# Logarithm of both parities of w, summed on TensorE, for steps 1 and 2 of a chunked RWKV kernel

## The chip, the cores and the metric

The kernel runs on one core of one Trainium2 chip. The metric is the device time of one execution in microseconds (us), as the median of several runs. A profile is one execution with the hardware profiler on. Engines are called by the profile's names: PE is TensorE (PEld its weight loads), ACT is ScalarE, DVE is VectorE, POOL is GpSimd, SP is the queue that issues all DMAs.

## The reference, cut to what matters

```python
# r, k, v, w: (4, 8, 768, 48), u: (8, 48); w lies between 0.8 and 0.95
for t in range(S):
    cur = einsum('bhd,bhe->bhde', u * k[t], v[t])
    y[:, :, t] = einsum('bhd,bhde->bhe', r[t], state + cur)
    state = w[t][..., None] * state + einsum('bhd,bhe->bhde', k[t], v[t])
x = y.transpose(0, 2, 1, 3).reshape(3072, 384)
out = maximum(x @ w_in, 0) ** 2 @ w_out      # w_in (384, 2048), w_out (2048, 384)
```

It is a linear attention with a decaying state for each head, and behind it a two-layer network with a squared ReLU. All inputs and the output are float32.

## The kernel before, in words

The sequence is worked on in 12 steps of 256 positions (4 batches of 3 steps). In a step two neighbouring positions (the two parities, j = 0 and 1) share one of 128 partitions, so a raw tile such as `w_raw` is 128 partitions x 8 heads x 2 parities x 48. The 256 positions of a step fall into two chunks of 64 partitions (c = 0 and 1).

What a step s does, by the names of its operations:

- `ww_` (line 272) multiplies the two parities of w, on the engine that the order names; `lw_` (line 276) takes the logarithm of the product on ACT into one of two buffers `lw_buf`, bf16, padded from 48 to 64 columns a head (the padding is zeroed once by POOL, lines 246 and 248).
- `cum_` (lines 332 to 336) sums the logarithms over the positions on PE: four small matmuls with two columns, which give the decay of a whole chunk, and two of 384 columns with triangular matrices. From step 3 on the second of these is left out, and `al_` on DVE derives it from the first; steps 0 to 2 do without `al_`. `exp_` (line 348) takes the exponential in PSUM, and `ac_` (line 354) that of the chunk decays.
- `rw_` and `kw_` (lines 294 and 298) move r and k by one parity, with POOL in the first steps. `rd_.s.1` (line 369, one instruction) and `rd_.s.0` (line 366, two halves) multiply k and r by the decays on DVE. `tr_` (line 382) transposes them on PE, and `rkt_` (line 396) copies them out of PSUM as kT (1) and rT (0).
- `p_` (line 422 or 425) multiplies kT and rT, `pm_` (lines 438 and 441) masks the product on DVE. `su_` (line 453), `ts_` and `sn_` (lines 461 to 468) carry the state on. `y_` and `yc_` (lines 490 and 502) make the output.
- The bonus term: `ku_` (line 305) is u times k, `qp_` (line 310) times r, `q_` (line 315) its sum, `qs_` and `vs_` (line 285) put that sum and v into rows of chunks, `vq_` (line 324) multiplies them, and `ysb_` (line 513) adds that to y. `v_` (line 280) casts v.
- The network: `yt_` and `xt_` (lines 525 and 530) transpose y, `m1_` (line 545) is the first layer, `rl_` (lines 554 and 556) the ReLU on ACT or DVE, `sq_` (lines 562 and 564) the square, `m2_` (line 576) the second layer, `os_` and `store` the output. `cast` (line 201) turns the loaded weights to bf16.
- `warm_.n.i.x` (line 596) issues n matmuls of 512 columns whose result nobody reads, into bank i.

The whole order of the work is written out by hand in the string `ORDER`. Its words are run one after the other: a word is an operation with its step, `=V`, `=A` or `=G` names DVE, ACT or POOL, and `:0`, `:m` and so on the PSUM banks. Every engine takes its own instructions strictly in that order; semaphores are set between engines where data or banks demand it. The loads of a step and of the weights are words too, and SP issues them in that order. PSUM has two pairs of banks for the attention (`att`), two banks `bk` and two banks `m1`.

Steps 0, 1 and 2 of the attention run at the start, ahead of the first `m1_`; what PE does between their operations there is `warm_`. From the first `m1_` on, attention and network are interleaved.

Of the kernel before, what the change touches and what calls it, by code (L numbers as in the profile page):

```python
# [22 lines left out]
ww_.2=G rkt_.1.1=A vs_.1.0=A lw_.2 v_.1=G y_.0:0 yc_.0.1 warm_.2.3.22 p_.1.1:1 p_.1.0:m warm_.6.1.7 vq_.0=G pm_.1.1
cum_.2:1 vs_.1.1=A pm_.1.0 qs_.1=A exp_.2 warm_.4.1.8 su_.1:m kw_.2=G ysb_.0=V rw_.2=G ts_.1.0=V warm_.1.0.23 y_.1:0
rd_.2.1 yc_.1.0 rd_.2.0 yt_.0:1 xt_.0=V sn_.1.0 cast.i.1=A vq_.1=G ts_.1.1=V warm_.1.0.24 tr_.2.1:2 yc_.1.1 ld.2.v
tr_.2.0:0 m1_.0.3:1 rkt_.2.1=A m1_.0.2:2 ac_.2 ysb_.1=V yt_.1:3 rkt_.2.0=A sn_.1.1 p_.2.1:1 rl_.0.3=A cast.i.0=V
p_.2.0:0 xt_.1=A ku_.2=V m1_.0.1:0 vs_.2.1=G m1_.1.0:3 m1_.1.2:1 vs_.2.0=A rl_.0.1=A m1_.1.1:0 v_.2=G rl_.0.2=A
rl_.1.0=A rl_.1.2=A qp_.2=G pm_.2.1 pm_.2.0 su_.2:1 rl_.1.1=V ts_.2.0=V ld.2.i m1_.0.0:2 m1_.1.3:1 cast.i.2=A y_.2:1
q_.2 yc_.2.0 sn_.2.0 yc_.2.1 rl_.1.3=A m1_.0.5:3 ld.3.i m1_.1.5:1 ld.3.w m1_.0.4:0 rl_.0.0=A rl_.0.5=V qs_.2=A
rl_.1.5=A cast.i.3=G m1_.1.7:3 ld.0.o m1_.1.4:1 vq_.2=V ysb_.2=V rl_.0.4=A rl_.1.7=A ww_.3=G cast.o.0=G m1_.0.7:2  # L30
yt_.2:3 ld.2.o m1_.0.6:0 lw_.3 cast.o.2=G cum_.3:1 xt_.2=V rl_.0.7=V ld.3.o m1_.2.4:3 rl_.0.6=V sq_.0.1=A ld.1.o
sq_.0.0=A rl_.1.4=A m1_.2.2:2 sq_.0.2=A m1_.1.6:0 m1_.2.7:1 ld.3.r rl_.1.6=A sq_.1.1=A rl_.2.2=V rl_.2.4=V m1_.2.5:2
rl_.2.7=V ld.3.k al_.3 rl_.2.5=V cast.o.1=V m1_.2.6:0 m2_.0.1.0:3 m2_.0.1.2 sq_.1.3=V kw_.3=G m1_.2.3:1 sq_.1.0=A
ld.3.v ld.5.w m2_.0.0.0:2 ac_.3 ld.4.w ld.4.r sq_.0.3=A rl_.2.6=A exp_.3 vs_.3.1=G ld.4.v ld.4.k m1_.2.0:0 m2_.0.0.2
m2_.0.1.1 cast.o.3=V rl_.2.0=A m1_.2.1:0 rw_.3=V m2_.0.1.3 rl_.2.3=A sq_.2.3=A rl_.2.1=A sq_.1.2=A rd_.3.0 m2_.0.0.1
os_.0.1=A tr_.3.0:0 rd_.3.1 m2_.0.0.3 tr_.3.1:1 ku_.3=V m2_.1.0.1:3 sq_.2.1=A os_.0.0=A m2_.1.0.0 rkt_.3.0=V
rkt_.3.1=V p_.3.0:0 v_.3=G p_.3.1:b su_.3:1 sq_.2.2=A vs_.3.0=A qp_.3=V ld.5.k ts_.3.0=A m2_.2.0.1:2 m2_.1.0.3
m2_.2.0.3 m2_.1.0.2 sq_.2.0=A ww_.4=G q_.3 pm_.3.0 lw_.4 qs_.3=A cum_.4:0 m2_.2.0.0 ld.6.w v_.4=A pm_.3.1 ww_.5=G
rw_.4=G sn_.3.0 ts_.3.1=V vq_.3=G ac_.4 al_.4 m2_.2.0.2 yc_.3.1:1 y_.3 m2_.2.1.0:1 m2_.2.1.2 os_.1.0=A kw_.4=V lw_.5
ysb_.3=V sn_.3.1 store.0.0 os_.2.0=A exp_.4 kw_.5=G rd_.4.1 rd_.4.0 cum_.5:1 ac_.5 yt_.3:3 xt_.3=A ld.5.r vs_.4.0=A  # L40
al_.5 store.0.1 ld.6.r m2_.2.1.3 m2_.2.1.1 os_.2.1=V m1_.3.0:3 rl_.3.0=A exp_.5 su_.4:0 m1_.3.1:2 rl_.3.1=A
m2_.1.1.3:0 m2_.1.1.1 dtr_.4.1 ku_.4=V rw_.5=V qp_.4=V m1_.3.7:2 rl_.3.7=A m1_.3.6:1 ts_.4.0=V dtr_.4.0 rl_.3.6=A
m2_.1.1.2 m1_.3.5:3 rd_.5.1 rl_.3.5=A m1_.3.4:1 sn_.4.0 ts_.4.1=V p_.4.0:0 q_.4 rd_.5.0 qs_.4=A ww_.6=G vs_.4.1=G
vq_.4=G rw_.6=G p_.4.1:1 sq_.3.0=V m2_.3.1.0:3 m2_.1.1.0 pm_.4.0 yc_.4.1:0 yc_.4.0 sq_.3.3=A m1_.3.3:2 rl_.3.4=A
sq_.3.2=A pm_.4.1 y_.4 lw_.6 m1_.3.2:1 rl_.3.3=A rl_.3.2=A cum_.6:1 m2_.3.0.2:2 m2_.3.0.3 sq_.3.1=A m2_.3.1.3
m2_.3.1.1 ku_.5=G qp_.5=G ld.5.v ysb_.4=V al_.6 ld.7.w ld.6.k ww_.7=G yt_.4:1 m2_.3.1.2 m2_.3.0.0 exp_.6 ac_.6
os_.1.1=V sn_.4.1 m2_.3.0.1 kw_.6=V rd_.6.0 rd_.6.1 dtr_.5.1 ld.6.v v_.5=G dtr_.5.0 xt_.4=A p_.5.1:1 store.2.0 ld.7.r
vs_.5.1=A os_.3.1=A lw_.7 su_.5:b p_.5.0:0 q_.5 v_.6=A store.2.1 ts_.5.0=V m1_.4.1:1 ku_.6=G rl_.4.1=A vs_.6.0=A
m1_.4.3:0 os_.3.0=A pm_.5.0 pm_.5.1 rl_.4.3=V m1_.4.2:3 rl_.4.2=A vs_.6.1=A qs_.5=G m1_.4.4:1 sn_.5.0 yc_.5.1:0
yc_.5.0 rl_.4.4=V su_.6:1 dtr_.6.0 m1_.4.7:0 rl_.4.7=A vs_.5.0=G dtr_.6.1 y_.5 m1_.4.6:1 ts_.6.0=V sn_.6.0 ld.9.w  # L50
m1_.4.5:3 m1_.4.0:2 vq_.5=V sq_.4.1=A rl_.4.6=A rl_.4.5=A sq_.4.2=A ysb_.5=V ts_.6.1=V rl_.4.0=V sq_.4.0=V yt_.5:0
m2_.4.1.1:1 xt_.5=A qp_.6=G q_.6 qs_.6=G ld.7.k p_.6.0:1 ld.8.v p_.6.1:m yc_.6.1:0 ld.7.v ld.8.r store.1.1 ld.8.w
vq_.6=G ku_.7=G pm_.6.1 sq_.4.3=A kw_.7=G m2_.4.1.0 m2_.4.1.2 m1_.5.1:0 rl_.5.1=A pm_.6.0 m2_.4.1.3 sn_.6.1 m1_.5.0:2
cum_.7:1 y_.6 m1_.5.7:3 vs_.7.0=A rl_.5.0=A os_.4.1=A ww_.9=V al_.7 m2_.4.0.0:0 rl_.5.7=V m1_.5.2:2 m1_.5.6:1 ww_.8=G
rw_.7=G exp_.7 ac_.7 m2_.4.0.1 vs_.7.1=G m2_.4.0.2 m1_.5.3:3 rl_.5.2=A sq_.5.0=A v_.7=A rl_.5.3=A m1_.5.5:2 sq_.5.1=A
ysb_.6=V vs_.8.0=G m2_.4.0.3 lw_.8 rl_.5.6=A rd_.7.1 qp_.7=V rd_.7.0 sq_.5.3=A su_.7:0 v_.8=G rl_.5.5=V rw_.8=V
m1_.5.4:3 rl_.5.4=V m2_.5.1.0:2 cum_.8:1 sq_.5.2=A ts_.7.0=V al_.8 q_.7 m2_.5.1.1 m2_.5.1.3 store.1.0 ld.8.k ld.11.k
ac_.8 store.3.1 dyt_.6 dtr_.7.1 dtr_.7.0 exp_.8 kw_.8=V sn_.7.0 ts_.7.1=V m1_.6.2:3 m2_.5.1.2 m1_.6.3:1 ld.9.r ld.10.w
sn_.7.1 os_.4.0=A rd_.8.1 m1_.6.1:0 os_.5.1=A ku_.8=G m1_.6.7:2 rd_.8.0 rl_.6.2=V ld.9.k rl_.6.3=A qs_.7=A m1_.6.4:1
su_.8:1 rl_.6.7=A p_.7.1:m p_.7.0:0 qp_.8=G rl_.6.1=V ts_.8.0=V yc_.7.1:1 yc_.7.0 rl_.6.4=A sq_.6.1=A m2_.5.0.2:0  # L60
m1_.6.6:1 store.3.0 rl_.6.6=A sq_.6.3=A dtr_.8.1 pm_.7.0 pm_.7.1 lw_.9 dtr_.8.0 m2_.5.0.1 m1_.6.5:2 y_.7 m1_.6.0:3
m2_.5.0.3 m2_.5.0.0 store.4.1 ku_.9=G q_.8 qs_.8=G ww_.10=G rl_.6.5=V vq_.7=V rl_.6.0=A vs_.8.1=A rw_.9=G sq_.6.0=A
p_.8.0:m p_.8.1:0 kw_.9=G qp_.9=G ysb_.7=V cum_.9:1 m2_.6.0.1:1 ld.9.v os_.5.0=A m2_.6.0.3 m2_.6.1.3:0 m2_.6.0.0
sq_.6.2=V m2_.6.0.2 m2_.6.1.0 sn_.8.0 al_.9 exp_.9 pm_.8.0 rd_.9.0 pm_.8.1 ld.10.k dyt_.7 v_.9=A ac_.9 m1_.7.7:2
y_.8:0 yc_.8.1 rd_.9.1 su_.9:1 vs_.9.1=A yc_.8.0 rl_.7.7=A m1_.7.4:3 ld.10.v vq_.8=G ysb_.8=V m1_.7.0:2 lw_.10
store.4.0 q_.9 rl_.7.4=A ts_.9.0=A rl_.7.0=A cum_.10:0 al_.10 vs_.9.0=V ac_.10 exp_.10 m2_.6.1.1 os_.6.0=V m2_.6.1.2
os_.6.1=A m1_.7.5:2 m1_.7.6:3 m1_.7.2:0 kw_.10=G dtr_.9.0 qs_.9=G rl_.7.5=A ld.10.r dyt_.8 sq_.7.2=A m1_.7.3:2
m1_.7.1:1 rl_.7.6=A dtr_.9.1 ld.11.w m1_.8.5:3 rl_.7.3=A rl_.7.1=A m1_.8.6:2 v_.10=G sn_.9.0 ts_.9.1=V rw_.10=G
rd_.10.1 rd_.10.0 ku_.11=G rl_.7.2=A rl_.8.5=V sq_.7.1=A ld.11.v m1_.8.7:1 p_.9.0:1 p_.9.1:0 m1_.8.1:3 store.6.1
vq_.9=G ww_.11=G ld.11.r vs_.10.1=G store.6.0 pm_.9.0 sn_.9.1 rl_.8.6=A rl_.8.7=A rl_.8.1=A lw_.11 m2_.7.1.2:0  # L70
m2_.7.1.1 pm_.9.1 kw_.11=V m1_.8.3:2 y_.9:0 yc_.9.1 su_.10:1 ysb_.9=V dtr_.10.0 m1_.8.4:1 sq_.7.3=A sq_.7.0=A
m2_.7.1.3 cum_.11:0 m2_.7.1.0 ts_.10.0=V rw_.11=V rl_.8.4=A rl_.8.3=V dtr_.10.1 ku_.10=G sq_.8.2=A ac_.11 os_.7.1=A
# [577 lines left out]
```

## Time and profile before

| | |
|---|---|
| median of 3 runs | 178.65 us (178.42 to 179.02) |
| the profiled execution's own time | 178.38 us |
| its span, first to last instruction | 176.6 us |
| busy in the span | PE 171.2, DVE 138.4, ACT 134.0, POOL 110.0 us |
| granted TensorE clock | full in all 40 slices of the span |

Busy times are sums of instruction durations. In a timeline line stand the start, the duration (from the first start to the last end, where several instructions are merged), the engine, the line, what is written from what, the count, and, in brackets, the idle time of the engine just before it with what ended it. The difference between span and time, 1.78 us, lies ahead of the first instruction and behind the last.

### The profile page before, as it was taken

To read this page: it belongs to the slowest core of one execution; us is meant where nothing else is said; L and a number is where in the kernel's file an instruction comes from. 1 tells how busy PE (TensorE), PEld (TensorE's weight loads), DVE (VectorE), ACT (ScalarE), POOL (GpSimd) and SP (SyncE) were. 2 spreads that over 40 slices of the span, in tenths; PEclk is the share of its full clock that TensorE was granted. 3 is DMA by queue.
4 is the path that set the end of the run, shared out by engine and by line. 5 is a ranking of instruction groups with operands and counts; after the bars stand their busy time and mean duration, and the time that the engine had idled before them with its cause. 6 is when DMAs were issued, how large, how long until landed. Compare 5 with 4: busy or idle time off the path is not lost.

```text
span 176.6 us, 5525 instructions
## 1 busy us (share of the span) xinstructions
PE 171.2 (97%) x2296; PEld 124.7 (71%) x2296; DVE 138.4 (78%) x205; ACT 134.0 (76%) x240; POOL 110.0 (62%) x132
## 2 busy tenths in 40 slices
...
GB/s 140 262 261 265 304 352 344 366 346 253 262 261 284 123 147 234 183 282 256 276 266 159 234 234 234 186 198 163 298 138 126 105 29 17 106 59 89 89 4 134
DMA packets 78954, 35.61 MB, mean 202 GB/s; under 512 B 72145, under 2 KB 77394, under 8 KB 78930
## 3 DMA queue, kind: packets, MB, share of 16 engines
...
## 4 chain that ended last, share of the span: by engine, by line
PE 91%; DVE 3%; DMA 2%; ACT 1%; issue 1%; DVEq 0%; ACTq 0%
PE m L545 19%; PE m L576 18%; PE bk L576 18%; PE bk L545 17%; PE att L490 3%; DMA w_raw<-in_w_dram 2%; PE m L596 2%; PE att L502 2%; PE att L453 2%; PE att L425 2%; PE bk L596 2%; DVE ww L272 1%; PE att L334 1%; PE bk L382 1%; PE att L332 1%
## 5 line engine op out<-in xcount | busy, mean ns | idle before, releaser
L545 PEld LDWEIGHTS <-wi_sb 128*128 128x128 bf16 x576 | 54.8, 98 | 10.0 <-DMA xT<-y_sb 0.2
L576 PEld LDWEIGHTS <-gt 128*128 128x128 bf16 x400 | 37.7, 98 | 19.5 <-ACT gt L562 0.2
L545 PE MATMUL m<-xT,wi_sb 128*128 128x256 bf16 x300 | 39.4, 273 | 0.0
L562 ACT ACTIVATE gt<-gt 128x1024 bf16<-128x1024 f16 x37 | 38.2, 1052 | 0.5
L545 PE MATMUL bk<-xT,wi_sb 128*128 128x256 bf16 x276 | 36.5, 273 | 0.0
L576 PE MATMUL bk<-wo_sb,gt 128*128 128x384 bf16 (+2 forms) x208 | 36.0, 314 | 0.0
L576 PE MATMUL m<-wo_sb,gt 128*128 128x384 bf16 x192 | 35.0, 326 | 0.0
L554 ACT ACTIVATE gt<-m 128x512 f16<-128x512 f32 x32 | 18.8, 595 | 11.0 <-PE m L545 10.6
L554 ACT ACTIVATE gt<-bk 128x512 f16<-128x512 f32 x36 | 21.0, 596 | 7.6 <-PE bk L545 7.4
L556 DVE TENSOR_SCALAR gt<-m 128x512 f16<-128x512 f32 x18 | 12.3, 687 | 13.0 <-PE m L545 12.6
L441 DVE TENSOR_TENSOR pmT<-att,mask 128x1024 bf16<-128x1024 f32 x16 | 19.1, 1215 | 1.1 <-PE att L425 0.9
L324 POOL TENSOR_TENSOR ku<-v_sh,qs 128x768 f32<-128x768 bf16 x9 | 13.3, 1475 | 8.6 <-ACT qs L285 8.5
L468 POOL TENSOR_TENSOR S<-t_state,ac_buf 128x192 bf16<-128x192 f32 x20 | 11.9, 595 | 10.0 <-DVE t_state L463 9.0
L305 POOL TENSOR_TENSOR ku<-k_raw,u_bc 128x768 f32<-128x768 f32 x9 | 16.7, 1855 | 0.6 <-DMA k_raw<-in_k_dram 0.6
L298 POOL TENSOR_TENSOR k_raw<-k_raw,w_raw 128x384 f32<-128x384 f32 x8 | 8.0, 1005 | 9.9 <-DMA k_raw<-in_k_dram 9.9
L513 DVE TENSOR_TENSOR y_sb<-att,ku 128x768 bf16<-128x768 f32 x12 | 11.5, 954 | 3.5 <-PE att L490 1.5
L369 DVE TENSOR_TENSOR kdec_buf<-k_raw,att 128x768 bf16<-128x768 f32 x12 | 11.4, 947 | 3.1 <-ACT att L348 3.1
L285 ACT CAST v_sh<-v_raw 64x384 bf16<-64x384 f32 x26 | 13.2, 509 | 0.3
L310 POOL TENSOR_TENSOR ku<-ku,r_raw 128x768 f32<-128x768 f32 x7 | 12.7, 1809 | 0.2
L366 DVE TENSOR_TENSOR rdec_buf<-r_raw,att 128x384 bf16<-128x384 f32 x24 | 12.2, 544 | 0.4 <-POOL r_raw L294 0.4
L285 POOL CAST v_sh<-v_raw 64x384 bf16<-64x384 f32 x18 | 10.6, 589 | 1.4 <-DMA v_raw<-in_v_dram 0.5
L315 DVE TENSOR_REDUCE q<-ku 128x16 f32<-128x768 f32 x12 | 11.3, 944 | 0.1
...
## 6 DMA issues: line engine op xcount, KB each, us to landing
...
kT<-kdec_buf SPq DMA_TRANSPOSE x8, 4.6
```

Source lines behind the costliest of these rows:

```text
L285: copy(out[j * Q:(j + 1) * Q, c], src[c * Q:(c + 1) * Q, :, j])
L305: tensor_mul("ku_", s, h)(tiles["ku", s][:, hs], raw["k", s][:, hs, 1:3, :], u_bc[:, hs, None, :].to_broadcast([C, n, 2, D]))
L310: tensor_mul("qp_", s, h)(ku, ku, raw["r", s][:, heads(h), 0:2, :])
L324: tensor_mul("vq_", s)(vq[:], tiles["vs", s][:], tiles["qs", s][:, :, :, None].to_broadcast([C, 2, H, D]))
L366: nc.vector.tensor_mul(rdec[0][:, ps, j, :, 0:D], x[:, :, j, :].rearrange("p (a e) d -> p a e d", e=2), dec.rearrange("p (a e) d -> p a e ...
L441: nc.vector.tensor_mul(pmT, ps_p[:].rearrange("p e (x t) -> p (e x) t", t=C), mk.to_broadcast([C, 8, C]))
L468: nc.gpsimd.tensor_mul(t[:], tiles.pop(("ts", s, c))[:].rearrange("p (a d) -> p a d", a=HP), tiles["a_c", s][:, :, c, None].to_broadcast([ ...
L545: nc.tensor.matmul(ps1[:, j, :], wi_sb[:, n // 4, kk, n % 4 * 128:(n % 4 + 1) * 128], tiles["xT", s][:, :, kk, :], start=(kk == 0), stop=( ...
L554: nc.scalar.activation(rl, m1, AF.Relu, scale=RS)
L556: nc.vector.tensor_scalar(out=rl, in0=m1, scalar1=RS, scalar2=0.0, op0=ALU.mult, op1=ALU.max)
L562: nc.scalar.activation(gt, rl, AF.Square)
L576: nc.tensor.matmul(m2, gt[:, 4 * q + n, rows * C:(rows + 1) * C], wo_sb[:, 4 * q + n, cols], start=(summed[s, c] == 1 and n == 0), stop=(s ...
```

## The change

Steps that have an `lw_` but no `ww_` in the order now take the logarithm of both parities in one ACT instruction, into one buffer `lw_pair` that steps 1 and 2 share, and each matmul of `cum_` becomes two, one for each parity, which add up in PSUM. `ww_.1` (on DVE) and `ww_.2` (on POOL) are gone. POOL zeroes `lw_pair` among the constants.

```diff
+    PAIR_LN = {steps with an lw_ word} - {steps with a ww_ word}
+    lw_pair = consts.tile([C, 2, H, DP], BF16)
         nc.gpsimd.memset(lw_bufs[1][:], 0.0)
+        if PAIR_LN:
+            nc.gpsimd.memset(lw_pair[:], 0.0)
     def lw_(s, h=None):
+        if s in PAIR_LN:
+            nc.scalar.activation(lw_pair[:, :, :, 0:D].rearrange("p j h d -> p h j d"), raw["w", s][:], AF.Ln)
+            return
     def cum_(s, h=None):
+        logs = [lw_pair[:, j] for j in range(2)] if s in PAIR_LN else [lw_bufs[s % NLW][:]]
...
         for p in pairs(h):
-            nc.tensor.matmul(cs[:, 0, DM + 2 * p:DM + 2 * p + 2], lw[:, 2 * p:2 * p + 2, :],
-                             half_ones[:], start=True, stop=True)
-        nc.tensor.matmul(cs[:, 0, 0:n], tri_strict[:], lw[:, hs, 0:D], start=True, stop=True)
-        if s not in ONE_SUM:
-            nc.tensor.matmul(cs[:, 1, 0:n], tri_incl_neg[:], lw[:, hs, 0:D], start=True, stop=True)
+            for lw, start, stop in zip(logs, ends["start"], ends["stop"]):
+                nc.tensor.matmul(cs[:, 0, DM + 2 * p:DM + 2 * p + 2], lw[:, 2 * p:2 * p + 2, :],
+                                 half_ones[:], start=start, stop=stop)
+        for into, tri in sums:
+            for lw, start, stop in zip(logs, ends["start"], ends["stop"]):
+                nc.tensor.matmul(into, tri[:], lw[:, hs, 0:D], start=start, stop=stop)
```

The order itself changes at these words and no others; between them it is the same:

| word | before | after |
|---|---|---|
| `ku_.0` | POOL, after `rw_.0` | DVE, after `rd_.0.0` |
| `ww_.1=V`, `ww_.2=G` | there | gone |
| `warm_.3.5.2` | after `rd_.0.0`, ahead of `tr_.0.0` | after `rd_.0.1`, ahead of `tr_.0.1` |
| `ac_.0` | after `p_.0.1`, behind `v_.0` on ACT | ahead of `rkt_.0.0` |
| `warm_.2.3.21` | between `tr_.1.0` and `tr_.1.1` | ahead of `warm_.5.5.3` and `p_.0.0` |
| `exp_.1` | after `vs_.0.0` on ACT | ahead of it (a cast of v) |
| `rd_.1.0`, `rd_.1.1` | in this order | the other way round |
| `vs_.1.0` | ACT | POOL |
| `vs_.1.1` | ahead of `qs_.1` on ACT | behind it |
| `warm_.1.0.23` | behind `su_.1` | ahead of `warm_.6.1.7` and `cum_.2` |
| `warm_.1.0.24` | ahead of `tr_.2.1` | ahead of `su_.1` |
| `warm_.4.1.8` | ahead of `su_.1` | behind it, ahead of `y_.1` |
| `qs_.2` | behind `rl_.0.0` | ahead of it |
| `m1_.3.3` | behind `m2_.3.1.0`, `pm_.4.0`, `yc_.4.1`, `yc_.4.0` | ahead of them |
| `rl_.6.5` | DVE | ACT |

More of the change, by code (lines that the diff above doesn't have):

```diff
@@ L23 @@
[L23 to L72, printed above, removed]
```

96 lines of the change are left out of this document (75 added, 21 removed).

## The prediction, on record before the run

> **What bounds the kernel now.** I read the page first, for busy shares, then the busy time by stretches, then the chain of waits, then the timeline of the first 27 us.
>
> ```profile
> span 176.6 us, 5525 instructions
> PE 91%; DVE 3%; DMA 2%; ACT 1%; issue 1%; DVEq 0%; ACTq 0%
> ```
> ```profile
> 25.00:30.00 5.00, 5.00 (x63) 4.37 (x61) 5.00 (x7) 4.94 (x10) 4.60 (x6) 1.00 1.09 361
> 100.00:105.00 5.00, 4.94 (x113) 4.04 (x111) 4.54 (x8) 4.00 (x9) 4.31 (x4) 1.00 1.22 261
> ```
> ```profile
> 9.21 1.59 DVE ww L272
> 25.29 0.71 PE bk L545 x6
> 103.05 0.36 DVE t_state L463
> ```
>
> The second line is the chain that ended last: 91% of it is PE. The stretch from 25 to 30 us has PE busy all 5.00 of 5 us at the full clock, and the one from 100 to 105, the only stretch between 15 and 170 us that is not full, still 4.94 (the chain puts the hole down to `ts_.8.0` at 103.05). So from the first `m1_` on, near 25.2, PE runs its own instructions back to back to the end. The edits of steps 1 and 2 lie ahead of that. They matter only by when the first `m1_` starts; the rest, 176.6 - 25.2 = 151.4 us, follows it one to one. The chain says where a gain could come from: `ww_.1` stands in it with 1.59 us, on DVE.
>
> **The change part by part. DVE.** These rows carry it.
>
> ```profile
> 3.12 0.53 POOL L248 MEMSET lw_buf<- 128x512 bf16 x1
> 4.56 0.56 DVE L272 TENSOR_TENSOR ww<-w_raw 128x384 f32<-128x384 f32 x1 [0.80 <-DMA w_raw<-in_w_dram]
> 8.58 1.81 POOL L305 TENSOR_TENSOR ku<-k_raw,u_bc 128x768 f32<-128x768 f32 x1
> 9.12 1.68 DVE L272 TENSOR_TENSOR ww<-w_raw 128x384 f32<-128x384 f32 x1
> 10.72 0.94 DVE L310 TENSOR_TENSOR ku<-ku,r_raw 128x768 f32<-128x768 f32 x1
> 12.21 1.01 POOL L298 TENSOR_TENSOR k_raw<-k_raw,w_raw 128x384 f32<-128x384 f32 x1 [1.82 <-DMA k_raw<-in_k_dram]
> ```
>
> The same product took 0.56 us alone and 1.68 while POOL worked on `ku_.0` (8.58 to 10.39). Removed: 1.59 us of DVE's chain. Added: `ku_.0` on DVE, of the size and type of `qp_.0` at 0.94, so 0.95. POOL's next work, `kw_.1`, waits for a DMA until 12.21, so nothing stands beside `ku_.0` there. DVE is 1.59 - 0.95 = 0.64 us earlier up to its next wait.
>
> The new memset of `lw_pair` is twice the size of the one at 3.12, so 2 x 0.53 = 1.06, from 3.65 to 4.71 on POOL, which has nothing to do then; it reaches 0.15 us into `ww_.0`, which is on the chain. If the two exclude each other that costs 0.15, else nothing; I take nothing, as the memsets at 3.12 kept their 0.53 beside DVE's own. [...]
>
> **ACT and PE up to p_.1.1.**
>
> ```profile
> 7.17 1.04 PE L596 MATMUL att<-warm 128*128 128x512 bf16 x4
> 8.33 0.62 PE L382 MATMUL bk<-ident,kdec_buf 128*128 128x128 bf16 x8
> 8.98 1.01 ACT L396 COPY kT<-bk 128x1024 bf16<-128x1024 bf16 x1 [1.24 <-PE bk L382]
> 10.08 1.01 ACT L396 COPY rT<-bk 128x1024 bf16<-128x1024 bf16 x1
> 10.99 0.83 ACT L280 CAST v_bf<-v_raw 128x768 bf16<-128x768 f32 x1
> 11.79 0.52 ACT L276 ACTIVATE lw_buf<-ww 128x384 bf16<-128x384 f32 x1
> 12.37 0.25 PE L332 MATMUL att<-half_ones,lw_buf 128*128 128x2 bf16 x4
> 12.64 0.32 PE L336 MATMUL att<-lw_buf,tri_incl_neg 128*128 128x384 bf16 x1
> 13.52 0.79 ACT L348 ACTIVATE att<-att 128x768 f32<-128x768 f32 x1
> 13.77 1.21 DVE L441 TENSOR_TENSOR pmT<-att,mask 128x1024 bf16<-128x1024 f32 x1
> 14.90 1.01 DVE L366 TENSOR_TENSOR rdec_buf<-r_raw,att 128x384 bf16<-128x384 f32 x2
> 15.82 0.95 DVE L369 TENSOR_TENSOR kdec_buf<-k_raw,att 128x768 bf16<-128x768 f32 x1
> 16.83 0.62 PE L382 MATMUL m<-ident,kdec_buf 128*128 128x128 bf16 x8
> 17.48 1.01 ACT L396 COPY kT<-m 128x1024 bf16<-128x1024 bf16 x1 [0.44 <-PE m L382]
> 18.56 0.40 PE L422 MATMUL att<-rT,kT 64*128 64x128 bf16 x8
> 19.28 1.21 DVE L441 TENSOR_TENSOR pmT<-att,mask 128x1024 bf16<-128x1024 f32 x1
> 19.12 1.47 PE L596 MATMUL bk<-warm 128*128 128x512 bf16 x6
> 22.30 0.39 PE L596 MATMUL bk<-warm 128*128 128x512 bf16 x1
> ```
>
> One warm matmul of 512 columns costs PE (1.47 - 0.39) / 5 = 0.216 us; 384 columns are then 0.16 and 128 are 0.054, by estimate. The four warms at 7.17 occupy PE to 8.03. `warm_.3.5.2` ahead of `tr_.0.1` keeps it to 8.68, where the transposes began at 8.33: 0.35 late. The kT copy goes from 8.98 to 9.33. Before, ACT idled some 0.1 us between its two copies, so the rT copy, `v_.0` and `ac_.0` (the last now first) slip by only 0.16, from the start of the rT copy to that of `lw_.1` still 11.79 - 10.08 = 1.71: `lw_.1` starts at 11.95 instead of 11.79.
>
> It has 768 elements now: bounded by 0.52 (no longer than with 384) and 1.04 (twice that); the cast of 128x768 beside it took 0.83, and I take that. It ends at 12.78, 0.47 later than before (12.31). That it no longer waits for `ww_.1` (done at 10.80) is worth nothing, since ACT came to it only at 11.79. `cum_.1` took 12.37 to 12.96, of which the four small matmuls and the first large one cost 0.27 of issue; six more cost 0.27 + 0.16 = 0.43 (bounds: nothing, and 0.59 again). So it ends at 12.78 + 0.06 + 0.59 + 0.43 = 13.86, and `exp_.1`, now ahead of `vs_.0.0`, starts at 13.90 instead of 13.52 and ends at 14.69. Moving it ahead is worth about 0.06 against before, where it waited for the cast, and the longer sum takes more than that.
>
> DVE is done with `pm_.0.1` at 14.90 - 0.64 = 14.26, and waits for `exp_.1` until about 14.78: 0.52 of its 0.64 are gone. The two decays last 15.82 + 0.95 - 14.90 = 1.87, to 16.65. `rd_.1.1` is first now, but PE's order still has `tr_.1.0` first, which needs the last half of `rd_.1.0`: seven transposes from 16.71, 0.38, and only then `tr_.1.1`, from 17.09 to 17.71, where it ended at 17.45 before. The kT copy, 17.74 to 18.75, and `p_.1.1` at 18.82: 0.26 later than 18.56. `pm_.1.1` starts when `p_.1.1` ends, at 19.28, as before. DVE's chain behind it, to `xt_.0`, keeps its place.
>
> **PE from p_.1.1 to the first m1_.**
>
> ```profile
> 20.55 0.24 PE L332 MATMUL att<-half_ones,lw_buf 128*128 128x2 bf16 x4
> 22.61 0.56 PE L490 MATMUL att<-v_sh,pmT 128*128 128x48 bf16 x16
> 24.61 0.68 PE L382 MATMUL bk<-ident,rdec_buf 128*128 128x128 bf16 x8
> 25.19 0.82 PE L545 MATMUL bk<-xT,wi_sb 128*128 128x256 bf16 x6
> ```
>
> Before, this took 25.19 - 18.56 = 6.63 us. PE waited in it three times: 0.13 before `cum_.2` (six warms from 19.12 end at 20.42, it began at 20.55, when `pm_.1.1` had read the bank), 0.09 before `y_.1` (22.30 + 0.22 to 22.61), and about 0.1 within `tr_.2.0` (0.58 from 24.61 to 25.19 against 8 x 0.054). The number of warms in it is 12 before and after; they are only dealt out otherwise, `warm_.4.1.8` behind `su_.1`. With `p_.1.1` late the three waits close, and `cum_.2` adds 0.43: 18.82 + 6.63 - 0.32 + 0.43 = 25.56 instead of 25.19. PE has then no slack left and sets the start of `m1_` itself, 0.37 late.
>
> **POOL and what comes later, at nothing.**
>
> ```profile
> 18.24 1.00 POOL L272 TENSOR_TENSOR ww<-w_raw 128x384 f32<-128x384 f32 x1
> 19.96 1.48 POOL L324 TENSOR_TENSOR ku<-v_sh,qs 128x768 f32<-128x768 bf16 x1
> 26.07 1.69 POOL L285 CAST v_sh<-v_raw 64x384 bf16<-64x384 f32 x2
> 105.34 0.60 ACT L554 ACTIVATE gt<-bk 128x512 f16<-128x512 f32 x1 [1.05 <-PE bk L545]
> ```
>
> POOL loses `ww_.2` (1.00) and gains `vs_.1.0`, two casts: at most 1.69, as at 26.07. What is queued behind is `v_.1`, `vq_.0`, `kw_.2`, `rw_.2`. `vq_.0` ended at 21.44 and DVE's `ysb_.0` needs it; at 1.69 it would come up to 0.69 late, DVE's chain with it, and by that chain the first `m1_` up to 0.5 late, a little more than PE's own 0.37. I take the casts as equal to `ww_.2`. `qs_.2` ahead of `rl_.0.0` and `m1_.3.3` ahead of `m2_.3.1.0` exchange work on engines where PE waits for nothing; `rl_.6.5` goes to ACT, which idled 1.05 there (105.34). If that cover is gone, each costs at most one instruction, 0.6.
>
> The sum: +0.37 us. From the profiled execution's 178.38 (span 176.6 and 1.78 around it) that is 178.75; the median, 178.65, lies 0.27 above that execution, so I forecast **179.0**. A measurement of this kernel can tell about 0.3%, 0.54 us, from no change, and 0.37 is under it.
>
> **Rivals.** *Faster: DVE stays the bound.* If the logarithm and the doubled sums cost near their lower bounds (0.52 and little), `exp_.1` ends by 14.17, DVE keeps its 0.64, and PE follows: 178.65 - 0.64 = **178.0**. For it: DVE has no idle time in the trace from 7.3 to 30 us, and `ww_.1` is in the chain. Against: it needs more than 0.52 of the 0.31 + 0.43 that I add on ACT and PE to be unreal. Chance 0.2.
>
> *Slower: the doubled sums at their upper bounds.* PE between `p_.1.1` and `m1_` has no slack once `p_.1.1` is later than about 18.5, and from there every delay of the path `lw_.1`, `cum_.1`, `exp_.1`, `tr_.1.1` goes through whole. With 1.04 for the logarithm (+0.21) and 0.59 for each doubled sum (+0.16 on the path and +0.16 again behind `p_.1.1`) that gives 0.37 + 0.53 = 0.90: **179.6**. It decides from +0.17 over my sum on. For it: the path has many small handovers, each of which I set at what it was before. Chance 0.35.
>
> *The change doesn't do what it says:* if `cum_` hides in PE's idle time and the words moved cancel, 178.65; that lies within my own case, whose chance is 0.45 with all that ends within 0.3%, its own range 178.3 to 179.2.
>
> **How the numbers follow.** The time is my own case's, 179.0. The range runs from the faster rival to the slower one's bound, 178.0 to 179.6, with about 0.1 left out at each end. Faster by over 0.3% (below 178.1): 0.2. Slower (above 179.2): 0.35. Within: 0.45.
>
> **What would show it.** Right: `lw_.1` near 0.83, `exp_.1` starting near 13.9, DVE idle some 0.5 ahead of `rd_.1.1` with ACT as releaser, `p_.1.1` near 18.8, no PE wait from there to the first `m1_` near 25.6, and PE full behind it. Wrong: the first `m1_` before 25.0, or DVE without that wait (the faster rival); a stretch after 26 us with PE not full, which would mean that the late words are not free; or `vq_.0` ending after 21.8 with `ysb_.0` waiting for POOL.

## The result, and the profile after

The changed kernel takes 179.82 us (median of 5 runs, 179.47 to 180.35), the kernel before 178.65: the ratio is 1.0074 [1.0057, 1.009]. It is slower, by about 1.3 us (0.0074 x 178.5), where 0.37 us and "within 0.3%" had been forecast, and above 179.6, the upper end of the forecast range. The profiled execution took 179.47 us, 1.09 more than that of before.

From the page of the changed kernel, its span, its chain of waits by engine and one group:

```profile
span 177.7 us, 5546 instructions
...
PE 76%; DVE 10%; DMA 7%; SPq 3%; issue 2%; POOL 1%; ACT 0%; DVEq 0%; POOLq 0%
...
L557 PEld LDWEIGHTS <-wi_sb 128*128 128x128 bf16 x576 | 54.8, 98 | 10.6 <-DMA xT<-y_sb 0.9
```

The chain was 91% PE and 3% DVE; it is now 76% PE, 10% DVE and 7% DMA. The third line is a weight load that waited 0.9 us for a DMA into `xT`.

Rows of its timeline up to the first `m1_`:

```profile
3.57 0.95 POOL L254 MEMSET lw_pair<- 128x1024 bf16 x1
...
4.40 0.56 DVE L278 TENSOR_TENSOR ww<-w_raw 128x384 f32<-128x384 f32 x1 [0.64 <-DMA w_raw<-in_w_dram]
...
8.96 0.95 DVE L314 TENSOR_TENSOR ku<-k_raw,u_bc 128x768 f32<-128x768 f32 x1
...
11.78 0.87 ACT L282 ACTIVATE lw_pair<-w_raw 128x768 bf16<-128x768 f32 x1
...
12.70 0.35 PE L345 MATMUL att<-half_ones,lw_pair 128*128 128x2 bf16 x8 [0.31 <-ACT lw_pair L282]
...
13.23 0.49 PE L349 MATMUL att<-lw_pair,tri_incl_neg 128*128 128x384 bf16 x2
...
13.82 0.80 ACT L360 ACTIVATE att<-att 128x768 f32<-128x768 f32 x1 [0.97 <-PE att L349]
...
14.70 0.95 DVE L381 TENSOR_TENSOR kdec_buf<-k_raw,att 128x768 bf16<-128x768 f32 x1 [0.49 <-POOL r_raw L303]
...
17.05 0.61 PE L394 MATMUL m<-ident,kdec_buf 128*128 128x128 bf16 x8
...
17.69 1.01 ACT L408 COPY kT<-m 128x1024 bf16<-128x1024 bf16 x1
...
18.59 0.38 PE L608 MATMUL m<-warm 128*128 128x512 bf16 x1 [0.16 <-issue]
...
18.90 0.45 PEld L434 LDWEIGHTS <-kT 64*128 64x128 bf16 x16 [0.42 <-ACT kT L408]
18.90 0.40 PE L434 MATMUL att<-rT,kT 64*128 64x128 bf16 x8
...
25.63 0.82 PE L557 MATMUL bk<-xT,wi_sb 128*128 128x256 bf16 x6
```

The first load landed 0.16 us earlier than in the execution of before, so everything here starts from 4.40 and not 4.56. Counted from `ww_.0`, the first `m1_` comes at 21.23 where it came at 20.63 (25.19 - 4.56): 0.60 late, of which the clock time shows only 0.44.

Busy time by stretches, behind it (after, then before):

```profile
25.00:30.00 5.00, 5.00 (x70) 4.41 (x70) 5.00 (x7) 4.89 (x9) 4.47 (x6) 1.00 1.08 360
...
50.00:55.00 5.00, 4.78 (x78) 3.08 (x76) 4.97 (x7) 4.70 (x10) 2.12 (x2) 1.00 1.23 275
...
110.00:115.00 5.00, 4.53 (x33) 2.63 (x33) 5.00 (x8) 4.02 (x7) 5.00 (x5) 1.00 1.33 223
```
```profile
50.00:55.00 5.00, 5.00 (x78) 3.15 (x76) 4.89 (x6) 4.91 (x13) 3.32 (x4) 1.00 1.22 273
...
110.00:115.00 5.00, 5.00 (x66) 3.28 (x68) 4.72 (x8) 3.91 (x8) 5.00 (x5) 1.00 1.27 199
```

The second column is PE's busy time in 5 us. Two holes are new, 0.22 us near 52 and 0.47 near 114, the sign that the forecast had named as "the late words are not free". The hole near 52, in the timelines of before and after:

```profile
48.19 0.95 DVE L305 TENSOR_TENSOR ku<-k_raw,u_bc 128x768 f32<-128x768 f32 x1
48.20 2.76 POOL L272 TENSOR_TENSOR ww<-w_raw 128x384 f32<-128x384 f32 x2 [0.47 <-DMA w_raw<-in_w_dram]
...
51.27 0.40 PE L422 MATMUL att<-rT,kT 64*128 64x128 bf16 x8
```
```profile
47.98 1.96 POOL L278 TENSOR_TENSOR ww<-w_raw 128x384 f32<-128x384 f32 x2
...
48.97 1.78 DVE L314 TENSOR_TENSOR ku<-k_raw,u_bc 128x768 f32<-128x768 f32 x1
...
52.01 0.40 PE L434 MATMUL att<-rT,kT 64*128 64x128 bf16 x8 [0.22 <-DVE kT L408]
```

`ku_.3` on DVE came 0.01 us ahead of POOL's two products and took 0.95 while POOL stretched to 2.76; now POOL is ahead, and DVE takes 1.78. The copy of kT behind it is late and PE waits 0.22 us. The hole near 114:

```profile
109.31 1.22 SPq L534 DMA_TRANSPOSE xT<-y_sb  x1
...
113.67 0.55 PEld L545 LDWEIGHTS <-wi_sb 128*128 128x128 bf16 x6 [0.25 <-DMA xT<-y_sb]
```
```profile
109.17 1.22 SPq L546 DMA_TRANSPOSE xT<-y_sb  x1
...
114.74 0.55 PEld L557 LDWEIGHTS <-wi_sb 128*128 128x128 bf16 x6 [0.86 <-DMA xT<-y_sb]
114.75 0.83 PE L557 MATMUL m<-xT,wi_sb 128*128 128x256 bf16 x6 [0.47 <-DMA xT<-y_sb]
```

`dyt_.7` transposes the y of step 7 by DMA into `xT` for `m1_.7.7`. Before, it landed about 4.3 us after its issue (113.6), and only the weight load waited for it, 0.25 us, which PE didn't feel. After, it was issued 0.14 earlier, took 5.5 us and landed at 114.7, and PE stood idle for 0.47 us. (Where something waits for it, the landing is 0.05 ahead of the waiting instruction's start.)

### The profile page after: what moved, and what is told of

Same layout as the page of the kernel before. It is cut to its first block, busy times and chain, and to the rows that moved or that the text cites. A ratio compares the mean times of both kernels' runs of the same rounds, so it can differ in the third digit from the quotient of the medians.

```text
span 177.7 us, 5546 instructions
## 1 busy us (share of the span) xinstructions
PE 171.7 (97%) x2305; PEld 125.5 (71%) x2308; DVE 138.8 (78%) x204; ACT 133.9 (75%) x239; POOL 109.0 (61%) x133
## 4 chain that ended last, share of the span: by engine, by line
PE 76%; DVE 10%; DMA 7%; SPq 3%; issue 2%; POOL 1%; ACT 0%; DVEq 0%; POOLq 0%
PE m L557 18%; PE bk L557 15%; PE m L588 14%; PE bk L588 14%; DMA k_raw<-in_k_dram 3%; DMA xT<-y_sb 3%; PE att L502 3%; SPq L182 2%; PE att L514 2%; PE att L465 2%; PE att L437 2%; PE bk L608 1%; DVE wo_sb L204 1%; PE att L349 1%; DVE gt L568 1%
## 5 line engine op out<-in xcount | busy, mean ns | idle before, releaser
L566 ACT ACTIVATE gt<-m 128x512 f16<-128x512 f32 x33 | 19.3, 593 | 11.7 <-PE m L557 11.6
L568 DVE TENSOR_SCALAR gt<-m 128x512 f16<-128x512 f32 x17 | 11.6, 687 | 13.1 <-PE m L557 12.5
L314 POOL TENSOR_TENSOR ku<-k_raw,u_bc 128x768 f32<-128x768 f32 x8 | 14.9, 1858 | 0.1
L294 POOL CAST v_sh<-v_raw 64x384 bf16<-64x384 f32 x20 | 12.2, 612 | 1.3 <-DMA v_raw<-in_v_dram 0.4
L294 ACT CAST v_sh<-v_raw 64x384 bf16<-64x384 f32 x24 | 12.2, 508 | 0.3
L360 ACT ACTIVATE att<-att 128x768 f32<-128x768 f32 x12 | 9.6, 800 | 2.8 <-PE att L349 2.4
```

The lines of the kernel that those rows point to most:

```text
L294: copy(out[j * Q:(j + 1) * Q, c], src[c * Q:(c + 1) * Q, :, j])
L314: tensor_mul("ku_", s, h)(tiles["ku", s][:, hs], raw["k", s][:, hs, 1:3, :], u_bc[:, hs, None, :].to_broadcast([C, n, 2, D]))
L566: nc.scalar.activation(rl, m1, AF.Relu, scale=RS)
L568: nc.vector.tensor_scalar(out=rl, in0=m1, scalar1=RS, scalar2=0.0, op0=ALU.mult, op1=ALU.max)
```

## The experiments

**Theory A** was that the head alone counts and the rest follows one to one, so that a late `m1_` costs what it is late and no more. **Its rivals** put the loss behind the first `m1_`: in the three late words (`qs_.2`, `m1_.3.3`, `rl_.6.5`), in the meeting of DVE and POOL near 49, or in the transpose near 109, which may be hurt by loads queued near it. Ratios are to the kernel before, timed in the same rounds. A hole, a landing or a late start is read from the one profiled execution of a kernel; its other executions may differ.

**e1: a delay alone.** On the kernel before, two warm matmuls (0.43 us) ahead of the first `m1_`.
```diff
-tr_.2.0:0 m1_.0.3:1
+tr_.2.0:0 warm_.2.1.30 m1_.0.3:1
```


> The kernel before, with two more warm matmuls of 512 columns directly ahead of the first m1_; nothing else differs, so PE's network part starts 0.43 us later (2 x 0.216). Theory A (the delay of the head is passed on one to one, and the later stalls of the changed kernel at 51 and 114 us need the changed kernel's own order): 178.65 + 0.43 = 179.1. Theory B (any delay of this size brings the later stalls with it, since DMA and GpSimd's loads keep their own times): 179.5 to 179.9, with PE stalls near 51 or 114 us. Theory C (the delay is absorbed by slack later): 178.65.

Measured: 1.003 [1.0016, 1.0044], some 0.54 us. The first `m1_` is 0.45 late from `ww_.0` and PE waits nowhere for `xT` (landed 4.0 us after its issue). A delay at that place is passed on, no more: for this edit theory A holds.

**e2: the changed kernel with the three late words as before.**
```diff
-m1_.0.4:0 qs_.2=A rl_.0.0=A rl_.0.5=V
+m1_.0.4:0 rl_.0.0=A rl_.0.5=V qs_.2=A
-sq_.3.0=V m1_.3.3:2 m2_.3.1.0:3 ... sq_.3.3=A
+sq_.3.0=V m2_.3.1.0:3 ... sq_.3.3=A m1_.3.3:2
-rl_.6.5=A
+rl_.6.5=V
```


> The changed kernel with the three late words (qs_.2, m1_.3.3, rl_.6.5) as before. Theory A (head and its consequences cost all): 179.8, as the changed kernel, with the stall on xT at 114 us still there. Rival L (the late words cost the 0.5 to 0.6 us that PE loses at 114 us waiting for the transposed y of step 7): 179.2, and PE full from 110 to 115 us.

Measured: 1.009 [1.007, 1.0111]. Nothing came back, and PE still waited 0.76 us for `xT`. The late words are not needed for the loss.

**e3: the kernel before with the three late words only** (the lines of e2 the other way round).


> The kernel before with the three late words as after, the head untouched. Theory A: 178.65, no difference. Rival L: 179.2, with a PE stall at 113 us.

Measured: 1.0051 [1.0035, 1.0066], with the first `m1_` where it was before (20.64 from `ww_.0`). The timeline:
```profile
108.99 1.21 SPq L534 DMA_TRANSPOSE xT<-y_sb  x1
...
114.84 0.83 PE L545 MATMUL m<-xT,wi_sb 128*128 128x256 bf16 x6 [0.74 <-DMA xT<-y_sb]
```
So the late words are enough to make the hole: issued 0.32 earlier than before, the transpose lands 1.2 later, and PE loses 0.74. My "nothing" for them falls.

**e4: the logarithm of both parities alone**, on the kernel before, no other word moved.
```diff
-tr_.0.0:1 ww_.1=V rkt_.0.0=A
+tr_.0.0:1 rkt_.0.0=A
-q_.1 ww_.2=G rkt_.1.1=A
+q_.1 rkt_.1.1=A
```


> The kernel before with the logarithm of both parities in steps 1 and 2 and the doubled sums, ww_.1 and ww_.2 gone, and no other word moved. By the rows of the two traces: the logarithm 0.87 instead of 0.52, each doubled sum 0.45 more, DVE 0.3 earlier since qp_.0 now waits for ku_.0 on GpSimd. Theory P (the pair itself costs PE its 0.45 behind p_.1.1 and little else): first m1_ at 25.1 to 25.4, 178.6 to 178.9. Rival Q (the pair costs as much as the whole head of the changed kernel): first m1_ near 25.6, 179.1 or more. Rival R (DVE's relief wins): first m1_ below 24.9, 178.3.

Measured: 1.0079 [1.0055, 1.0104]. The first `m1_` is 0.49 late, and PE then waits 1.15 us for `xT`. The pair of logarithms has both losses by itself.

**e5 and e6: the loads around the transpose.** On the changed kernel, `ld.10.v` behind `dtr_.9.0` (e5), so that it isn't queued directly behind the transpose, or `ld.10.k` behind `dyt_.7` (e6), so that it isn't ahead of it. (`ld.10.v` and `ld.10.k` load v and k of step 10; `dtr_.9.0` is the DMA transpose of step 9's r.)
```diff
-m1_.7.4:3 ld.10.v vq_.8=G ... dtr_.9.0
+m1_.7.4:3 vq_.8=G ... dtr_.9.0 ld.10.v
```
```diff
-pm_.8.1 ld.10.k dyt_.7
+pm_.8.1 dyt_.7 ld.10.k
```


> The changed kernel with the load of v for step 10 issued behind the DMA transpose of step 9's r instead of directly behind the transpose of step 7's y (xT). In the five traces so far xT took 4.0 to 4.3 us from issue to landing where it was issued 2.7 us or more behind the load of k for step 10, and 5.2 to 5.8 where it came 2.2 to 2.6 behind it. Theory D1 (the v load behind it goes ahead of part of the transpose): xT lands in 4.0 to 4.3, PE is full from 110 to 115 us, 0.5 to 0.7 us less than the changed kernel, 179.2. Theory D2 (the k load ahead of it holds it): xT still 5.2 or more, 179.8. Ratio to the kernel before by D1 1.004, by D2 1.0075.

> The changed kernel with the load of k for step 10 issued behind the transpose of step 7's y instead of ahead of it. Theory D1 (a load behind the transpose takes its place): xT no better, 5 us or more, ratio to before 1.0075 or worse. Theory D2 (the k load ahead of it holds it): xT lands in 4.0 or less, PE full from 110 to 115, ratio 1.004, 179.2.

Measured: e5 1.0046 [1.0027, 1.0065], PE waits 0.34; e6 1.0038 [1.0022, 1.0055], PE doesn't wait, its weight load does:
```profile
114.04 0.55 PEld L557 LDWEIGHTS <-wi_sb 128*128 128x128 bf16 x6 [0.29 <-DMA xT<-y_sb]
```
With the hole gone there, e6 costs 0.68 us, about the 0.61 by which its first `m1_` is late (its twelve executions range from 178.58 to 180.12). It is the best kernel with the change whole.

**e7: the meeting near 49.** On the changed kernel, `ku_.3` behind `rkt_.3.1`.
```diff
-tr_.3.1:1 ku_.3=V m2_.1.0.1:3
+tr_.3.1:1 m2_.1.0.1:3
-rkt_.3.1=V p_.3.0:0
+rkt_.3.1=V ku_.3=V p_.3.0:0
```


> The changed kernel with the bonus product of step 3 on VectorE behind the copies of rT and kT of step 3 instead of ahead of them. In the changed kernel that product took 1.78 us beside GpSimd's product of w for step 5, where it took 0.95 before, and the copies behind it were late, so that PE waited 0.22 at 52 us. Theory K (that meeting costs 0.2 to 0.3): PE full from 50 to 55 us, ratio to the kernel before 0.0013 lower than the changed kernel's 1.0074, 179.5. Rival N (the 0.2 is made up later by slack, so that nothing comes of it): 179.8.

Measured: 1.0083 [1.0061, 1.0105]. `ku_.3` takes 0.95 and the stretch from 50 to 55 is full, but nothing is gained, since PE waits 0.76 us at 115 instead. Nor does this show that the slow product made the hole: e5, e6 and e9, with the same words there as the changed kernel, have that stretch full too, and in e6 `ku_.3` takes 1.78 us as in the changed kernel. In e1, e11, e14 and e15, with the head of before, it is slow as well (1.32 to 1.76), and that stretch is full. The hole near 52 stood in one execution and is not a cost of the change as such.

**e8: the moved words alone**, with `ww_.1` and `ww_.2` put back into the changed kernel.
```diff
-tr_.0.0:1 ac_.0
+tr_.0.0:1 ww_.1=V ac_.0
-q_.1 rkt_.1.1=A
+q_.1 ww_.2=G rkt_.1.1=A
```


> The changed kernel with the products of w of steps 1 and 2 put back at the places they had (VectorE and GpSimd), so without the pair: every word move, logarithm and sums as before. Theory P2 (the pair itself costs the head 0.45 and the moves nothing): first m1_ 20.6 to 20.8 us behind the first product of w, as before (20.63), ratio to before 1.002 to 1.005 with the late stalls. Rival M (the moves cost the head): 21.2 as in the changed kernel, 1.0075.

Measured: 1.0077 [1.0051, 1.0102]. The first `m1_` is 0.67 late with no doubled sum at all, though `exp_.1` starts earlier (8.67 after `ww_.0`; before 8.96): DVE has `ku_.0` and `ww_.1` both. PE waits 0.49 for `xT`.

**e9: a cover.** On the changed kernel, one word of the second layer, of step 6, ahead of `m1_.7.7`.
```diff
-ac_.9 m1_.7.7:2
+ac_.9 m2_.6.1.1 m1_.7.7:2
```


> The changed kernel with one second-layer group, m2_.6.1.1 (four matmuls, 0.65 us of PE work that needs nothing new), moved ahead of m1_.7.7, the first user of the transposed y of step 7 (xT), whose landing PE waited for by 0.47. Theory X (the part of the loss that the head does not explain is PE waiting for xT): no PE wait for xT, ratio to before 1.003 to 1.005, 179.0 to 179.3. Rival S (the wait only moves to the next transfer or operation): 1.007, 179.7.

Measured: 1.0055 [1.0035, 1.0075]. The hole shrinks to 0.04, and a new one of 0.27 opens at 120, where PE waits for an output copy.

**e10: one late word.** The kernel before with `rl_.6.5=A` and nothing else.


> The kernel before with rl_.6.5 on ScalarE and nothing else changed. With all three late words the kernel before took 1.0051 of its time, and PE waited 0.7 us for xT, whose transpose was issued 0.3 us earlier and landed 1.2 us later. Theory V (rl_.6.5 does that alone, since it lets VectorE finish y of step 7 earlier and the transpose is issued closer behind the load of k): xT takes 5.2 us or more, ratio 1.004 to 1.006. Rival W (one of the other two words does it): ratio 1.000 to 1.001, xT 4.0 to 4.5.

Measured: 1.0040 [1.0024, 1.0056]. The transpose is issued at 108.62, 0.69 earlier than before, takes 5.5 us and lands at 114.1, and PE waits 0.47. One ReLU moved from DVE to ACT, where the cast behind it starts at 108.34 (108.32 in before), goes with the hole: DVE gets to `ysb_.7` earlier (107.64; 108.32 in before) and the transpose is issued sooner, and yet it lands later. Why an earlier issue should land later, this run does not show (see Open, below).

**e11 and e12: late words with the cover, and the head put right.** e11 is e3 with the cover of e9. e12 is the changed kernel with the cover, the late words as before, and three words of the head:
```diff
-ld.0.v warm_.3.5.2 tr_.0.1:0 ... tr_.0.0:1
+ld.0.v tr_.0.1:0 ... warm_.3.5.2 tr_.0.0:1
-tr_.1.0:0 rkt_.1.0=V tr_.1.1:2
+tr_.1.1:2 tr_.1.0:0 rkt_.1.0=V
-warm_.4.1.8
+warm_.2.1.8
```


> The kernel before with the three late words and with m2_.6.1.1 ahead of m1_.7.7. Theory X (what the late words cost is PE's wait for xT): ratio 0.999 to 1.001. Rival S: 1.004 or more.

> The changed kernel with its head mended and the late part covered: warm_.3.5.2 back behind tr_.0.1, tr_.1.1 ahead of tr_.1.0, two warm matmuls fewer behind su_.1, the three late words as before, m2_.6.1.1 ahead of m1_.7.7. Theory H (the head is a chain over ScalarE and PE, lw_.1 to p_.1.1, with PE serial behind it): p_.1.1 about 0.5 to 0.7 us earlier, first m1_ 20.7 to 20.9 us behind the first product of w (21.23 in the changed kernel, 20.63 before), ratio to before 0.999 to 1.002. Rival G (GpSimd's vq_.0 and kw_.2 take over as the bound of the head): first m1_ still 21.1 or more, ratio 1.003 or more.

Measured: e11 1.0036 [1.0023, 1.0048], e12 1.0034 [1.0023, 1.0045]. In e12 the first `m1_` is back (20.68 from `ww_.0`), with the doubled logarithm and sums still there: its delay was a matter of the order around them and of two warm matmuls. The three words were changed together; the two warm matmuls by themselves are 2 x 0.216 = 0.43 us of PE's time, of the 0.55 that came back. Both keep a hole of 0.26 between 115 and 120.

**e13 to e16: nothing queued behind the transpose.** `ld.10.v` and `store.4.0` behind `dtr_.9.0`, in the changed kernel (e13), in the kernel of e10 (e14), in the kernel before (e15, the control), and in the changed kernel with the head of e12 (e16, late words as changed, no cover).
```diff
-m1_.7.4:3 ld.10.v vq_.8=G ... lw_.10 store.4.0 q_.9 ... dtr_.9.0
+m1_.7.4:3 vq_.8=G ... lw_.10 q_.9 ... dtr_.9.0 ld.10.v store.4.0
```


> The changed kernel with both transfers that were issued directly behind step 7's y transpose (the load of v for step 10 and a store of step 4) moved behind the next transpose. Theory D3 (transfers behind the transpose go ahead of its last packets): xT lands 4.0 to 4.3 us after its issue, no PE wait for it, ratio to before 1.003 to 1.005, the head's 0.45 to 0.6 alone. Theory D2 (the k load ahead holds it): xT 5.2 or more, ratio 1.0075.

> The kernel before with rl_.6.5 on ScalarE (1.0040, xT 5.5 us, PE wait 0.5) and both transfers moved as in the run on the changed kernel. Theory D3: xT 4.0 to 4.3, no wait, ratio 0.999 to 1.001. Theory D2: xT 5.2 or more, ratio 1.004.

> The kernel before with both transfers moved behind the next transpose, nothing else. Theory D3: xT at 4.0 to 4.3 as before, ratio 0.998 to 1.000. Theory D2: the same, so this is the control for what the two moved transfers cost elsewhere; a ratio over 1.002 would mean that moving them costs by itself.

> The changed kernel with the mended head (warm_.3.5.2 behind tr_.0.1, tr_.1.1 ahead of tr_.1.0, two warm matmuls fewer behind su_.1), which began m1_ 20.68 us behind the first product of w instead of 21.23, and both transfers moved, late words as in the changed kernel. Theory D3 and H: no PE wait for xT, ratio 0.998 to 1.002, about the kernel before. Theory D2: ratio 1.004, xT 5.2 or more.

Measured: e13 1.0119 [1.0093, 1.0144], e14 1.0050 [1.0038, 1.0063], e15 1.0033 [1.0021, 1.0044], e16 1.0048 [1.0032, 1.0064]. That what is queued behind delays the transpose falls with e14: with nothing directly behind, it took 6.1 us. In e14 the DMA engines were nearly empty before it landed (the last columns of the stretches are the DMA share and GB/s), where before they were full:
```profile
113.00:114.00 1.00, 0.67 (x5) 0.20 (x2) 1.00 (x2) 0.85 (x2) 1.00 (x3) 1.00 0.18 36
```
```profile
113.00:114.00 1.00, 1.00 (x9) 0.60 (x7) 1.00 (x2) 0.97 (x2) 1.00 (x2) 1.00 1.23 281
```
The two moves cost 0.33% by themselves (e15), so they repair nothing. The profiled execution of e13, 179.56, is its fastest, 1.1 under its median, and tells nothing of where the rest went.

**e17 and e18: step 7 without the DMA transpose.** y of step 7 is transposed by PE and copied by ACT, in the changed kernel (e17) and in the kernel before (e18).
```diff
-m2_.6.0.2 m2_.6.1.0 ... pm_.8.0 rd_.9.0 ... ld.10.k dyt_.7
+... pm_.8.0 yt_.7:3 m2_.6.0.2 m2_.6.1.0 rd_.9.0 ... ld.10.k xt_.7=A
```


> The changed kernel with y of step 7 transposed by TensorE and copied by ScalarE, as steps 0 to 5 do, instead of by a DMA transpose; two second-layer groups are moved behind the mask product so that the bank is free. PE pays 0.34 us for six transposes. Theory X (head 0.45 plus xT's wait 0.5 to 0.6 are the loss): ratio to the kernel before 1.004 to 1.006, and 0.002 to 0.0035 above the same edit on the kernel before. Rival S (other waits take its place): 1.008 or more.

> The kernel before with the same edit for step 7. PE pays 0.34 us: ratio 1.001 to 1.003. Theory X: 0.002 to 0.0035 below the changed kernel with the same edit (the head alone). Rival S: 0.006 or more below it, as without the edit.

Measured: e17 1.0075 [1.0062, 1.0089], e18 1.0032 [1.0019, 1.0045]. Neither waits for an `xT`. The difference, 0.0043 or 0.73 us between the medians (179.88 and 179.15), is what the change costs where that transpose can't play a part: about its late first `m1_` (0.60). Against the 1.17 between the medians of the two kernels themselves, some 0.4 belongs to the transpose; with intervals of 0.0013 either way on both ratios that is an estimate.

**All runs in one table.** "Late" is the start of the first `m1_` from `ww_.0`, less 20.63; "hole" is PE's idle time between 110 and 125 us; "cost" is the ratio less 1, times 178.5. All in us; "issued" and "landed" are those of the transpose of step 7.

| run | late | hole | sum | cost | issued | landed |
|---|---|---|---|---|---|---|
| before | 0 | 0 | 0 | 0 | 109.31 | 113.6 |
| after | 0.60 | 0.47 | 1.07 | 1.32 | 109.17 | 114.7 |
| e1 | 0.45 | 0 | 0.45 | 0.54 | 109.95 | 114.0 |
| e2 | 1.18 | 0.75 | 1.93 | 1.61 | 110.08 | 115.3 |
| e3 | 0.01 | 0.74 | 0.75 | 0.91 | 108.99 | 114.8 |
| e4 | 0.49 | 1.15 | 1.64 | 1.41 | 109.50 | 115.1 |
| e5 | 0.61 | 0.34 | 0.95 | 0.82 | 109.16 | 114.6 |
| e6 | 0.61 | 0 | 0.61 | 0.68 | 109.03 | 114.0 |
| e7 | 0.60 | 0.76 | 1.36 | 1.48 | 109.33 | 115.1 |
| e8 | 0.67 | 0.49 | 1.16 | 1.37 | 109.36 | 114.9 |
| e9 | 0.67 | 0.31 | 0.98 | 0.98 | 109.02 | 114.8 |
| e10 | 0.01 | 0.47 | 0.48 | 0.71 | 108.62 | 114.1 |
| e11 | -0.01 | 0.26 | 0.25 | 0.64 | 108.57 | 114.2 |
| e12 | 0.05 | 0.32 | 0.37 | 0.61 | 109.04 | 114.2 |
| e13 | 0.60 | 0.29 | 0.89 | 2.12 | 109.44 | 114.3 |
| e14 | 0.01 | 1.06 | 1.07 | 0.89 | 108.57 | 114.7 |
| e15 | 0.02 | 0.12 | 0.14 | 0.59 | 109.40 | 113.6 |
| e16 | 0.31 | 1.11 | 1.42 | 0.86 | 108.75 | 114.9 |
| e17 | 1.32 | 0.15 | 1.47 | 1.34 | none | none |
| e18 | 0.01 | 0.15 | 0.16 | 0.57 | none | none |

Late and hole come from one profiled execution each, the cost from medians. In 13 of the 19 kernels other than before the sum and the cost agree within 0.25 us. In e11, e15 and e18, whose words near 110 were rearranged, 0.39 to 0.45 of the cost is left over. e2 and e16 cost less than their sum by 0.32 and 0.56; their profiled executions, 180.07 and 179.65, were 0.19 and 0.40 above their medians. e13 is not explained. None of these kernels beats the one before.

The hole near 52 is not in the column. With it the profiled execution of the changed kernel is accounted for: 0.60 + 0.22 + 0.47 = 1.29, where its own time was 1.09 above that of before and hid 0.16 by the earlier first load.

## Why the prediction was wrong, step by step

**Right.** `lw_.1` took 0.87 (0.83 was taken), `ku_.0` 0.95 (0.95); the memset of `lw_pair` (0.95, from 3.57 to 4.52) lay beside the start of `ww_.0` at 4.40 and cost it nothing, 0.56 as before. DVE waited 0.49 ahead of `rd_.1.1` (0.5 was said; the profile names POOL as releaser, but `exp_.1` ended last, at 14.62), so it did not stay the bound, and the faster rival is out. `cum_.1` lasted 1.02, from 12.70 to 13.72, as summed (0.59 + 0.43). The stretch from `p_.1.1` to `m1_` took 25.63 - 18.90 = 6.73 (6.74 was summed, with 0.1 for a wait that by its own figures, 0.58 - 0.43, is 0.15). The casts on POOL took 1.06, and `vq_.0` ended at 21.41 (21.44 before).

**Mis-sized: the delay of `p_.1.1`.** Set from `ww_.0`, it is 0.50 late, where I had 0.26. Of the missing 0.24, 0.08 stands ahead of `exp_.1` (9.42 after `ww_.0`; 13.90 - 4.56 = 9.34 was summed), 0.03 in the transposes and the copy, and 0.13 between the end of the kT copy (18.70) and `p_.1.1` (18.90), 0.20 where I kept the 0.07 of before. A matmul of `warm_.2.3.22`, ahead of it in PE's order, began only at 18.59, which is the likely reason. The profiled execution hid 0.16 of it by an earlier first load.

**The step that failed: "the rest" that "follows it one to one", with the late words "at nothing".** From the first `m1_` to the end the kernel before took 151.4 us, and the forecast kept that. The changed kernel took 177.7 - 25.6 = 152.1: 0.7 more, its two holes (0.22 + 0.47). PE was full from 25 us on in the trace of before, and I took that for a chain with nothing else near it. The transpose of step 7 was as near as could be. The page of before has the line:

```profile
L545 PEld LDWEIGHTS <-wi_sb 128*128 128x128 bf16 x576 | 54.8, 98 | 10.0 <-DMA xT<-y_sb 0.2
```

A weight load had waited 0.2 us for `xT`; PE was at the 24 matmuls of `m2_` meanwhile (109.75 to 113.81 in the timeline). Almost no slack was left: in the traces in which PE itself waits for `xT`, its idle time is the wait of the weight load less 0.38 or 0.39 (0.86 and 0.47 in the changed kernel, 1.53 and 1.15 in e4, 0.72 and 0.34 in e5), so the 0.25 of before left some 0.13, by estimate, and a landing later than that is PE's idle time. It landed later after nearly every edit: with the late words alone (e3, 0.74 us lost), with one of them (e10, 0.47), and with the logarithms alone (e4, 1.15). "Which idled 1.05 there" was true of ACT and beside the point: moving `rl_.6.5` did not cost ACT anything, it let DVE finish y of step 7 sooner, and the transpose was issued sooner. My ceiling for a late word, "at most one instruction, 0.6", looked at the engine and not at the DMA behind it. The sign that I had named, a stretch that is not full, does not by itself point at the late words either: e2 and e4 have the hole without them. That a late head shifts everything evenly is shown only for e1.

**The slower rival** gave nearly the time measured, 179.6, by another way: the doubled sums were not at their upper bounds. The loss is some 0.6 to 0.7 us of head (e6: 0.68 with no hole, e17 against e18: 0.73) and some 0.4 to 0.5 of transpose (its hole, 0.47; the medians, 1.17 - 0.73). The rest of the 1.32, about 0.2, isn't assigned: in the profiled execution the hole near 52 makes it up, and in others the late start of the next paragraph may.

**One more thing that the head lost.** In e18 and e14, with the head of before, `exp_.0` came 0.28 and 0.45 late from `ww_.0` (2.15 and 2.32 for 1.87), and the first `m1_` still at 20.64: PE and ACT had that much slack beside DVE. The timeline of e18:

```profile
4.57 0.56 DVE L272 TENSOR_TENSOR ww<-w_raw 128x384 f32<-128x384 f32 x1 [0.81 <-DMA w_raw<-in_w_dram]
...
6.72 0.80 ACT L348 ACTIVATE att<-att 128x768 f32<-128x768 f32 x1 [0.97 <-PE att L336]
...
25.21 0.81 PE L545 MATMUL bk<-xT,wi_sb 128*128 128x256 bf16 x6
```

In e2 and e17, with the changed head, a start 0.54 late came out at `m1_` as 0.58 and 0.72 more than in the changed kernel. The change spent PE's and ACT's slack to free DVE, which was the bound only up to that slack. Executions of e17 with that start can also be part of the 0.73.

**Open.** Why the transpose lands so late. Its own issue alone does not set it. Issued 1.8 to 3.0 us behind `ld.10.k`, the load ahead of it in SP's order, it landed 6.9 to 7.0 us behind the issue of that load in three executions (before, e1, e13) and 7.8 to 8.0 behind it in the other thirteen with the load at about its usual time; in e15, where the load was issued about 1.3 us sooner, it was 8.2. So the landing goes with the load ahead, an earlier issue of the transpose mostly makes its own time longer, and what is open is the one microsecond between the two groups. Before and e1 have the latest issues of these sixteen, 2.69 and 2.96 behind the load, but e13 landed early too, issued 2.03 behind it.

The traces show sixteen signals for the landing of the transpose, with the time of each. In before, e1, e6, e13 and e15 all came within 0.15 us. In eleven others fifteen came together and the last 0.85 to 1.7 us behind them, in the changed kernel at 113.12 and 114.70; in e7 and e9 all sixteen were late. What held the last one is not shown. A 16 KB load of instructions runs near it in every execution, 5.6 to 5.7 us behind `ld.10.k` in ten of the thirteen late ones, but 4.0 to 4.4 behind it in the other three as in the three early ones: a candidate for part of it, and no more. It is not what is queued behind (e5 5.4, e14 6.1). Taking the load of k from ahead of the transpose went with a landing at 114.0 in one execution (e6); that both loads were held back wasn't tried.
